# Attention feeding an FFN on one core: value loads ahead of plain casts, paired scores in the second batch, and a new set of order biases

## The chip, the cores and the metric

The kernel runs on one core of a Trainium2 chip. Times are device microseconds of one execution, lower is better. Every number comes from one profiled execution of the kernel before, from its run times, or from answers of its trace.

## The reference

Eight batches of eight heads, 576 positions, head size 64. Heads 0 to 3 attend to a plain window of 32, heads 4 to 7 to a window of 32 with steps of 4 ("dilated"). The result, laid out as tokens by 512 columns, goes through a two-layer FFN with a gate.

```python
mask_plain = (rel >= 0) & (rel < window)                       # window = 32
mask_dil = (rel >= 0) & (rel < window * dilation) & (rel % dilation == 0)   # dilation = 4
scores = np.where(masks, q @ k.T / 8, -1e9)
attn = softmax(scores)
x = (attn @ v).transpose(0, 2, 1, 3).reshape(4608, 512)
h = x @ w_in                                                   # 512 -> 2048
out = (h / (1 + np.exp(-beta * h))) @ w_out                    # 2048 -> 512
```

## The kernel before

Everything is an entry of a list of operations (`plan.op`). Each has the engines that may run it with a cost in ns, what it depends on, a due time `vt`, and the PSUM banks it takes. When all are listed, `Plan.run` plays them through a model: at each step it takes, for each engine, the operation with the smallest `vt` among those that could start nearly first, and writes it into that engine's program. `NUDGE` adds a bias in ns, by the number of the operation in the list, to the start that this choice compares. So the order on every engine is fixed when the program is built, and each engine then works through its own list, strictly in order. Where the model sees PE (TensorE) idle in the first 80 us, it puts in a matmul on zeros (`filler`, L1040), which keeps PE active.

A tile of the FFN is 512 tokens, a batch of attention 576, so nine tiles follow eight batches. For tile t, `slot_h` makes 16 blocks of h (L892, four matmuls of 512 columns each), tanh on ACT (L901) and the gate on DVE (L906); `block` multiplies by `w_out` (L927) and stores. Attention of batch b = t + 1 is spread between the FFN work of tile t by its due times.

How q, k and v of a batch get in depends on b:

- b = 0, 1, 2 (`b < DIRECT`): POOL's queue loads q and k as bf16 into `st`, PE transposes them (L474, L484), and ACT or DVE copies them to kT, qT (plain heads) and dk, dq (dilated heads).
- b = 3 to 7: POOL's queue casts q and k into scratch in DRAM (`cast`, four DMAs: k and q dilated, k and q plain), and SP's queue brings each back with a transposing DMA (`crossbar`, L465). A tiny copy on POOL, `pace` (L1006), holds all of this back until xT of batch b - 2 has arrived.
- The values: `direct_vd` loads the dilated heads' values (into `vd16`, or into `st` from b = 3), which the copy `spread` (L248) moves to vd, and twice a tail into `vt_`; `direct_vp` loads the plain heads' values into vp, after which the copy `halo` (L248) fills 32 rows of it. Either copy may stand on DVE, POOL or, for `spread`, ACT.

Scores are half-height matmuls (L688 dilated, L752 and L716 plain), and "T" is the tail of the dilated heads (L657). ACT takes exp (L624). For b = 0 the mask was added before by PE (L678, L738, L741), for others a multiply on DVE or POOL applies it (L628). Then come the values (L793 dilated, L809 plain, L778 the tail "U") and the normalisation on DVE (L643, L644) into xdm, xsp and xdt. For b = 0 and 1 PE transposes the result into xT; from b = 2 (`BY_DMA`) SP stores it to DRAM rows (L511, L519, L524) and fetches it with a transposing DMA into xT, in two halves (L538).

From b = 2 (`PAIRED`) one score operation handles two heads or pairs of heads; from b = 3 (`AT_ONCE`) all plain scores are one.

In `loads`, for b >= 3, the due times put the four casts at b - 2 to b - 1.97 and the values at b - 1.98 and b - 1.97:

```python
for n, (z, h0) in enumerate(((0, 4), (1, 4), (0, 0), (1, 0))):
    c = cast(b, z, h0, [go], b - 2 + .01 * n)
...
ld[b]["vd"] = direct_vd(b, [go] + war(*key), b - 2 + .02, [go] + war(("vt", b % 2)))
ld[b]["vp"] = direct_vp(b, [go] + war(("vp", b % 2)), b - 2 + .03)
```

On POOL's queue a batch of this kind is: k dilated, q dilated, k plain, vd, two vt, q plain, vp.

Of the kernel before, what the change touches and what calls it, by code (L numbers as in the profile page):

```python
# [39 lines left out]
class Plan:  # L40
# [3 lines left out]

    CAPS = {"h": 3, "p": 4, "o": 2, "z": 4, "a": 8, "s": 5, "w": 6}
    SWITCH = 95
    NUDGE = {10: 900, 16: -150, 32: -150, 34: 400, 40: -900, 65: -150, 99: -150, 121: -900, 159: -400,
        165: -400, 190: -150, 215: 400, 222: -400, 362: 900, 382: -900, 422: -900, 426: -150,
        443: 900, 537: 400, 553: -400, 656: -150, 836: 400, 838: 400, 881: -150, 914: -60,
        1113: 400, 1133: -900, 1136: 400, 1158: -400}  # L50
    LAT = {"PE": 210, "ACT": 45, "DVE": 45, "POOL": 60, "SP": 0}
    NEAR = {"PE": 40, "ACT": 60, "DVE": 60, "POOL": 60, "SP": 0}

# [3 lines left out]
    def op(self, engs, fn, deps=(), vt=0.0, acquire=None, group=None, dma=0, lat=None, halves=False, sbuf=False):  # L57
        acquire = acquire if acquire is None or isinstance(acquire, list) else [acquire]
        o = Op(engs, fn, deps, vt, acquire, group or acquire, dma, lat, halves, sbuf)
        o.bias = self.NUDGE.get(len(self.ops), 0)  # L60
        self.ops.append(o)
# [128 lines left out]
def kernel(  # L190
# [12 lines left out]
    B, H, S, D = q.shape  # L203
# [20 lines left out]
    DV = 80  # L224
    DIRECT = 3
    ADDED = 1
    PAIRED = 2
    BY_DMA = 2
    APART = 4
    AT_ONCE = 3  # L230
# [12 lines left out]
    def bank(g, dt=FP32):  # L243
        b = BANKS[g.bank][:]
        return b if dt == FP32 else b.bitcast(BF16)
# [50 lines left out]
    vd = [const([P, 4, C, DV], BF16, f"vd{i}") for i in range(2)]  # L296
    vt_ = [const([2 * KTL, 2, 4, DV], BF16, f"vt{i}") for i in range(2)]
# [38 lines left out]
    fill3 = plan.op([("DVE", 500)], t_fill3, vt=-7.8)  # L336
# [61 lines left out]
    def dma(queue, out, in_):  # L398
        {"POOL": nc.gpsimd, "SP": nc.sync}[queue].dma_start(out=out, in_=in_)  # L399

    def load(queue, args, deps, vt, kb, rate=.4, issue=750, lat=1100):
        return plan.op(
            [(queue, issue)],
            lambda e: dma(queue, *args), deps, vt, dma=kb * 1024 / rate / 1000, lat=lat)

    def direct_qk(b, z, h0, deps, vt):
        rows, n, dst = ((2 * GD, RD, std) if h0 else (P, RP, stp))
        src = bass.AP(tensor=(k, q)[z].tensor, offset=(k, q)[z][b, h0].offset,
                      ap=[[n * D, rows], [2 * S * D, 2], [1, n * D]])
        return load("POOL", (dst[z], src), deps, vt, 576, .41 if b else .33, lat=1100 if b else 1000)  # L410

    def first_keys():

        stage = g_t[1][0:2 * GD, 0:6, :].rearrange("p f n -> p (f n)").bitcast(FP32).rearrange("p (x e) -> p x e", x=2)
        src = bass.AP(tensor=k.tensor, offset=k[0, 4].offset,
                      ap=[[RD * D, 2 * GD], [2 * S * D, 2], [1, RD * D]])
        o = load("SP", (stage, src), [], -9.1, 576, .41, 400, 1200)
        return [plan.op([("ACT", 175 + .834 * RD * D), ("DVE", 160 + 1.042 * RD * D)],
                        lambda e, x=x: copy(e, std[0][:, x], stage[:, x]), [o], -9.1, sbuf=True) for x in range(2)]

    def direct_vp(b, deps, vt):

        out = []
        rows = vp[b % 2][:].rearrange("p (h i) d -> p h i d", h=4)
        for hs in ((slice(0, 4),) if b else (slice(0, 2), slice(2, 4))):
            n = hs.stop - hs.start
            src = bass.AP(tensor=v.tensor, offset=v[b, hs.start].offset, ap=[[D, QT], [QT * D, n * NI], [1, D]])
            o = load("POOL", (vp[b % 2][WIN:P, hs.start * NI:hs.stop * NI, 0:D], src), deps, vt, n * 144, .27,
                     1150 if b else 750, 1100 if b < DIRECT else 5500)

            def halo(e, hs=hs):
                copy(e, rows[0:WIN, hs, 1:NI, 0:D], rows[QT:P, hs, 0:NI - 1, 0:D])
            out.append(plan.op([("DVE", 160 + .27 * n * 320), ("POOL", 170 + 1.04 * n * 320)], halo, [o],
                               b - 1 if b else -2.5, sbuf=True))
        return out

    def direct_vd(b, deps, vt, tdeps=()):
        src = v[b, 4:8].rearrange("h (t T) d -> t h (T d)", T=C)[0:P]
        out = [load("POOL", (vd16_of[b].rearrange("p h T d -> p h (T d)"), src), deps, vt, 512, .35, lat=1100 if b < DIRECT else 4000)]
        for c in range(2):  # L440
            src = bass.AP(tensor=v.tensor, offset=v[b, 4].offset + ((P - WIN) * C + c) * D,
                          ap=[[2 * D, 2 * KTL], [S * D, 4], [1, D]])
            out.append(load("POOL", (vt_[b % 2][:, c, :, 0:D], src), list(tdeps), vt + (1.255 if b == 0 else .02 if b < DIRECT else 0) + .001 + .001 * c, 96, .2, lat=1100 if b < DIRECT else 4000))
        return out

    scratch = {}
# [1 line left out]
    def cast(b, z, h0, deps, vt):  # L448

        dst = scratch[b, z, h0] = dram_pool.tile([S * 4 * D], BF16, name=f"s{b}_{z}_{h0}")  # L450
        src = (k, q)[z][b, h0:h0 + 4]
        if h0:
            args = [x.rearrange("(a c e) -> c a e", c=16, e=1024) for x in (dst[:], src.rearrange("h s d -> (h s d)"))]
        else:
            args = (dst[:].rearrange("(s h d) -> s h d", h=4, d=D), src.rearrange("h s d -> s h d"))
        return load("POOL", args, deps, vt, 576, .38 if h0 else .2, 500 if h0 else 1700)
# [37 lines left out]
    def war(*keys):  # L494
        return [o for key in keys for o in last.get(key, ())]
# [4 lines left out]
    def wrote(*keys):  # L500
        for key in keys:
            last[key] = []
# [39 lines left out]
    def attention(b, ld, names, vts):  # L542
# [106 lines left out]
        for name in [n for n in names if n[0] in "ST"]:  # L649
# [19 lines left out]
            x = int(name[1])  # L669
            if b >= PAIRED and x % 2:  # L670
                continue
            xs = (x, x + 1) if b >= PAIRED else (x,)
            gs = [Group("s") for _ in range(2 * len(xs))]
# [279 lines left out]
    ld = {b: {} for b in range(B)}  # L953
    for n, (z, h0) in enumerate(((0, 4), (1, 4), (0, 0), (1, 0))):
        ld[0]["qk", z, h0] = first_keys() if n == 0 else direct_qk(0, z, h0, [], -9 + .01 * n)
    ld[0]["vd"] = direct_vd(0, [], -8.5, [fill3])
    ld[0]["vp"] = direct_vp(0, [fill3], -8.4)
    for n, (c0, c1) in enumerate(((0, 512), (512, 1024), (1024, 2048))):
        o = load("POOL", (w_in_bf[:, :, c0:c1], moe_w_in[:, c0:c1].rearrange("(c p) d -> p c d", p=P)),
# [11 lines left out]
    def t_identf(e):  # L971
# [6 lines left out]
        out=beta_half[:], in_=bank(gb)[:, 0:NFB], scalar=0.5, op=ALU.mult), [bt], -1.4, group=gb)  # L978
# [8 lines left out]
    def xready(lo, hi, kts=range(NKT)):  # L987
        return [o for ks, a, b, o in xcopy if a < hi and b > lo and set(kts) & set(ks)]

    def loads(b):  # L990
        if b < DIRECT:
            base = -7.25 if b == 1 else .2
            for n, (z, h0) in enumerate(((0, 4), (1, 4), (0, 0), (1, 0))):
                ld[b]["qk", z, h0] = direct_qk(b, z, h0, war(("st", z)), base + .01 * n)
            wrote(("st", 0), ("st", 1))
            ld[b]["vd"] = direct_vd(b, war("vd16"), base + .05, war(("vt", b % 2)) + [fill4])
            wrote("vd16", ("vt", b % 2))
            ld[b]["vp"] = direct_vp(b, war(("vp", b % 2)) + [fill4], base + .06)
            wrote(("vp", b % 2))
        else:  # L1000
            behind = [ld[b - 1]["x", z, h0] for z in range(2) for h0 in (0, 4)] if b > DIRECT else []

            mid = (b - 2) * S + S // 2

            def t_pace(e, b=b, mid=mid):
                nc.gpsimd.tensor_copy(out=pace[:], in_=(  # L1006
                    xT[0:1, 0, mid - 1:mid + 1] if b - 2 >= BY_DMA else g_t[b % 2][0:1, 0, 0:2]))
            go = plan.op([("POOL", 150)], t_pace, behind + (
                xready(mid - 1, mid + 1) if b - 2 >= BY_DMA else gop[b - 2, 0]), b - 2.4)
            for n, (z, h0) in enumerate(((0, 4), (1, 4), (0, 0), (1, 0))):  # L1010
                c = cast(b, z, h0, [go], b - 2 + .01 * n)
                key = [(((("dk", "dq") if h0 else ("kT", "qT"))[z]), b % 2, i) for i in range(2)]
                ld[b]["x", z, h0] = crossbar(b, z, h0, [c] + war(*key), b - 2 + .01 * n)
                wrote(*key)
            key = [("st", z) for z in range(2)] if b < DIRECT + 2 else [("st", b % 2)]
            ld[b]["vd"] = direct_vd(b, [go] + war(*key), b - 2 + .02, [go] + war(("vt", b % 2)))
            wrote(("st", b % 2), ("vt", b % 2))
            ld[b]["vp"] = direct_vp(b, [go] + war(("vp", b % 2)), b - 2 + .03)
            wrote(("vp", b % 2))

    steady = LATER.split()
    for t in range(NTT):
# [4 lines left out]
        b = t + 1  # L1027
# [46 lines left out]
```

## Time and profile before

| | us |
|---|---|
| median of three runs | 302.39 |
| the three runs | 512.2, 301.24, 302.39 |
| the profiled execution, its own time | 302.39 |
| its span, first to last instruction | 300.7 |
| PE busy | 294.7 |
| fillers on PE (L1040, 65 matmuls) | 11.0 |
| DVE busy, ACT busy, POOL busy | 183.2, 171.3, 90.5 |

The span is what the trace covers; the execution's own time holds some start and end besides. A row of the trace gives start, duration, engine, line, operation and tiles, and in brackets how long the engine stood idle before it and what ended that.

### The profile page before, as it was taken

To read this page: it belongs to the slowest core of one execution; us is meant where nothing else is said; L and a number is where in the kernel's file an instruction comes from. 1 tells how busy PE (TensorE), PEld (TensorE's weight loads), DVE (VectorE), ACT (ScalarE), POOL (GpSimd) and SP (SyncE) were. 2 spreads that over 40 slices of the span, in tenths; PEclk is the share of its full clock that TensorE was granted. 3 is DMA by queue.
4 is the path that set the end of the run, shared out by engine and by line. 5 is a ranking of instruction groups with operands and counts; after the bars stand their busy time and mean duration, and the time that the engine had idled before them with its cause. 6 is when DMAs were issued, how large, how long until landed. Compare 5 with 4: busy or idle time off the path is not lost.

```text
span 300.7 us, 6078 instructions
## 1 busy us (share of the span) xinstructions
PE 294.7 (98%) x2342; PEld 150.2 (50%) x2342; DVE 183.2 (61%) x415; ACT 171.3 (57%) x311; POOL 90.5 (30%) x130
## 2 busy tenths in 40 slices
PE   8999999999999989999999999999999999999995
PEld 5765556445554435544444544455444444444454
DVE  4769778787858716886477746685781543343300
ACT  3868864857457643865585546754852554555311
POOL 8997363852127204600733074110000000000000
PEclk9999999999999999999999999999999999999999
DMA  8999999799979998999899989996024000100122
GB/s 168 184 211 201 207 190 207 114 143 171 201 201 149 161 161 207 180 148 230 148 191 147 211 164 161 163 183 170 0 74 116 36 36 35 37 35 35 57 85 70
DMA packets 111248, 41.98 MB, mean 140 GB/s; under 512 B 87620, under 2 KB 104596, under 8 KB 111220
## 3 DMA queue, kind: packets, MB, share of 16 engines
q0 software_dynamic: 60336, 18.58, 60.1%
q1 hardware_dynamic: 50740, 22.95, 37.9%
q8 instruction: 18, 0.29, 0.4%
q10 hardware_dynamic: 144, 0.07, 0.1%
q14 instruction: 10, 0.08, 0.1%
HBM read 37.76 MB, written 18.87 MB: 188 GB/s over the span
## 4 chain that ended last, share of the span: by engine, by line
PE 83%; DMA 9%; POOL 2%; SPq 2%; issue 1%; DVE 1%; ACT 0%; POOLq 0%
PE bank L892 36%; PE bank L927 35%; DMA vp<-in_v_dram 6%; PE bank L1040 2%; DMA xT<-x 2%; PE bank L809 1%; PE bank L793 1%; PE bank L688 1%; SPq L465 1%; DMA x<-xsp 1%; PE bank L716 1%; PE bank L484 1%; PE bank L474 1%; PE bank L752 1%; POOL s L399 1%
## 5 line engine op out<-in xcount | busy, mean ns | idle before, releaser
L927 PE MATMUL bank<-w_out_bf,g 128*128 128x512 bf16 (+2 forms) x608 | 140.2, 368 | 0.0
L901 ACT ACTIVATE tnh<-bank,beta_half 128x512 bf16<-128x512 f32 x144 | 98.1, 689 | 71.2 <-PE bank L892 67.6
L906 DVE SCALAR_TENSOR_TENSOR g<-tnh,bank 128x512 bf16<-128x512 bf16 x144 | 97.2, 685 | 66.6 <-ACT tnh L901 66.0
L892 PE MATMUL bank<-xT,w_in_bf 128*128 128x512 bf16 (+1 forms) x584 | 137.6, 376 | 0.0
L892 PEld LDWEIGHTS <-w_in_bf 128*128 128x128 bf16 x584 | 55.4, 98 | 61.5
L927 PEld LDWEIGHTS <-g 128*128 128x128 bf16 x608 | 55.0, 98 | 56.2
L942 ACT ACTIVATE osb<-bank 128x512 f32<-128x512 f32 (+1 forms) x34 | 20.0, 589 | 32.8 <-PE bank L927 32.0
L624 ACT ACTIVATE pt<-bank 128x384 bf16<-128x384 f32 (+1 forms) x54 | 20.4, 465 | 5.3 <-PE bank L716 3.2
L624 ACT ACTIVATE ptd<-bank 128x512 bf16<-128x512 f32 x32 | 16.8, 604 | 4.8 <-PE bank L688 4.7
L644 DVE TENSOR_TENSOR xsp<-bank,rcp 96x384 bf16<-96x384 f32 x32 | 17.7, 554 | 1.1
L628 DVE TENSOR_TENSOR pt<-pt,mask_n 128x384 bf16<-128x384 bf16 (+1 forms) x39 | 13.0, 349 | 7.0 <-ACT pt L624 6.5
L643 DVE RECIPROCAL rcp<-bank 96x6 f32<-96x6 f32 (+2 forms) x72 | 12.9, 179 | 6.8 <-PE bank L809 3.4
L399 POOL DMA_DIRECT2D vp<-in_v_dram x9 | 15.2, 1695 | 1.3 <-DMA vp<-in_v_dram 1.3
L1006 POOL COPY pace<-xT 1x2 bf16<-1x2 bf16 x4 | 0.7, 176 | 47.7 <-DMA xT<-x 47.7
L628 DVE TENSOR_TENSOR ptd<-ptd,mask_d 128x512 bf16<-128x512 bf16 x27 | 11.0, 423 | 5.8 <-ACT ptd L624 5.0
L644 DVE TENSOR_TENSOR xdm<-bank,rcp 128x256 bf16<-128x256 f32 x32 | 13.6, 424 | 1.1
L399 POOL DMA_DIRECT2D s<-in_q_dram x10 | 13.6, 1358 | 0.0
L399 POOL DMA_DIRECT2D vt<-in_v_dram x16 | 13.3, 1000 | 0.0
L1040 PE MATMUL bank<-zero 128*128 128x256 bf16 x65 | 11.0, 314 | 1.1 <-DVE warm L307 1.1
L399 POOL DMA_DIRECT2D s<-in_k_dram x10 | 11.1, 1106 | 1.5 <-issue 1.1
L809 PEld LDWEIGHTS <-pt 128*128 128x128 bf16 x192 | 8.9, 97 | 4.9 <-DVE pt L628 0.2
L944 DVE TENSOR_SCALAR osb<-bank 128x512 f32<-128x512 f32 (+2 forms) x4 | 2.1, 525 | 14.5 <-PE bank L927 14.5
(111 smaller groups left out, 182.7 us busy)
## 6 DMA issues: line engine op xcount, KB each, us to landing
out_dram<-osb SPq DMA_DIRECT2D x35, 256.0 KB, 2.5
s<-in_k_dram POOLq DMA_DIRECT2D x10, 288.0 KB, 6.7
s<-in_q_dram POOLq DMA_DIRECT2D x10, 288.0 KB, 10.0
w_out_bf<-in_moe_w_out_dram POOLq DMA_DIRECT2D x2, 1024.0 KB, 16.2
vp<-in_v_dram POOLq DMA_DIRECT2D x7, 288.0 KB, 17.1
st<-in_q_dram POOLq DMA_DIRECT2D x6, 288.0 KB, 12.9
x<-xsp SPq DMA_DIRECT2D x12, 144.0 KB
st<-in_k_dram POOLq DMA_DIRECT2D x5, 288.0 KB, 14.2
```

The source lines that it names most:

```text
L399: {"POOL": nc.gpsimd, "SP": nc.sync}[queue].dma_start(out=out, in_=in_)
L624: nc.scalar.activation(out=w(), in_=sc(), func=ACT.Exp, scale=SCALE)
L628: E[e].tensor_tensor(out=w(), in0=w(), in1=m(), op=ALU.mult)
L643: nc.vector.reciprocal(out=r, in_=p[..., D])
L644: nc.vector.tensor_tensor(out=dst, in0=p[..., 0:D], in1=r.unsqueeze(len(p.shape) - 1).to_broadcast(list(p.shape[:-1]) + [D]), op=ALU.mult)
L809: nc.tensor.matmul(pv[:, a, h2, :], lhsT=lhs, rhs=vp[kv][:, (2 * x + h2) * NI + 3 * j + a, 0:D + 1], start=True, stop=True)
L892: nc.tensor.matmul(bank(g)[:, a:z], lhsT=w_in_bf[:, kt, fb * P:(fb + 1) * P], rhs=xT[:, kt, xo + a:xo + z], start=(i == 0 and kt == kts[0] ...
L901: nc.scalar.activation(out=th[:, 0:n], in_=bank(g)[:, 0:n], func=ACT.Tanh, scale=beta_half[:, fb:fb + 1])
L906: nc.vector.scalar_tensor_tensor(out=g_t[t % 2][:, fb, c0:c0 + n], in0=th[:, 0:n], scalar=1.0, in1=bank(g)[:, 0:n], op0=ALU.add, op1=ALU.mult)
L927: nc.tensor.matmul(bank(g)[:, lo:hi], lhsT=g_t[t % 2][:, fb, tb * P:(tb + 1) * P], rhs=w_out_bf[:, fb, lo:hi], start=(fb == 0), stop=(fb = ...
L942: nc.scalar.mul(out=ob[:, lo:hi], in_=bank(g)[:, lo:hi], mul=0.5)
L1040: nc.tensor.matmul(BANKS[b][:, 0:256], lhsT=zero[:, 0:P], rhs=zero[:], start=True, stop=True)
```

## The change

Four edits:

1. `NUDGE` is replaced: 30 biases of up to 900 ns become 110 of up to 2500 ns.
2. `PAIRED` goes from 2 to 1, so that the scores of b = 1 are made in pairs too. This also renumbers the operations that come after.
3. In `loads`, for b >= 3, the due times of the two plain casts grow by .03, to b - 1.95 and b - 1.94, past the values at b - 1.98 and b - 1.97.
4. In batch 0 the vd load's due time goes from -8.5 to -8.985, and the constant for the tails grows by .485, so that their own due time stays.

```diff
-    NUDGE = {10: 900, 16: -150, 32: -150, 34: 400, 40: -900, 65: -150, 99: -150, 121: -900, 159: -400,
...
+    NUDGE = {7: -900, 16: -2500, 17: -150, 19: -2500, 32: -400, 36: 900, 55: 900, 57: 900, 58: -2500,
+        70: 400, 71: 900, 81: -150, 85: -2500, 89: -2500, 94: -150, 113: -150, 114: -150,
...
-    PAIRED = 2
+    PAIRED = 1
...
-... vt + (1.255 if b == 0 else .02 if b < DIRECT else 0) + .001 + .001 * c, 96, .2, ...
+... vt + (1.7399999999999993 if b == 0 else .02 if b < DIRECT else 0) + .001 + .001 * c, 96, .2, ...
...
-    ld[0]["vd"] = direct_vd(0, [], -8.5, [fill3])
+    ld[0]["vd"] = direct_vd(0, [], -8.985, [fill3])
...
-                c = cast(b, z, h0, [go], b - 2 + .01 * n)
+                c = cast(b, z, h0, [go], b - 2 + .01 * n + (0 if h0 else .03))
```

What comes out on POOL's queue in the changed program, by batch (line numbers of the changed kernel are ten higher from the planner on):

| b | order of the loads after pace |
|---|---|
| 3 | q dilated, k dilated, vd, vt, vt, vp, k plain, q plain |
| 4 | k dilated, q dilated, vt, vt, vp, k plain, q plain, vd |
| 5 | q dilated, k dilated, vd, vt, vp, k plain, q plain, vt |
| 6 | k dilated, q dilated, vd, vt, vt, vp, k plain, q plain |
| 7 | k dilated, q dilated, vd, vt, vp, k plain, q plain, vt |

The copies move as well: in b = 4 the halo copy of vp goes from DVE to POOL and the spread copy of vd from POOL to DVE, where it stands ahead of the masks of that batch. On SP, qT's transpose of b = 3 now comes ahead of both stores of xsp of b = 2 instead of between other stores. In the opening POOL builds add_d and issues the vd load of b = 0 ahead of ident_b.

## The prediction

> **What bounds the kernel now.** I read the page's parts 1 and 2 first, then the waits of PE (TensorE), the chain of waits around the one PE wait that is not in the opening, DVE's timeline there, and last the DMA share of that stretch.
>
> ```profile
> span 300.7 us, 6078 instructions
> PE 294.7 (98%) x2342; PEld 150.2 (50%) x2342; DVE 183.2 (61%) x415; ACT 171.3 (57%) x311; POOL 90.5 (30%) x130
> ...
> PEclk9999999999999999999999999999999999999999
> DMA  8999999799979998999899989996024000100122
> ...
> PE bank L793 <- DVE ptd L628: 1.3, 1, 1.3
> PE bank L1040 <- DVE warm L307: 1.1, 1, 1.1
> PE bank L678 <- POOL add_d L350: 0.3, 1, 0.3
> ```
>
> PE is the bound, at full clock. Because the ends of matmuls are modelled, 98% alone proves little, so I laid PE's own instruction order end to end: columns / 2.4 ns plus 2.5 for a wide matmul (four of 512 columns take 0.86 us in the chain of waits), the spacing of starts in the timeline for the narrow ones, and 95 ns wherever half-height scores meet full-height work (0.97 instead of 0.86 us after each score). The sum puts the last matmul at 294.4 us; the trace has it at 297.4. The 3.0 us of difference arise in two places: 2.0 in the first 17 us, and 1.4 at 111 to 113 us. Elsewhere PE never waits. Besides, 65 matmuls on zeros (L1040, 11.0 us busy) fill gaps that the planner expected. That is all there is to win.
>
> The second place, by the chain of waits and then the timelines of DVE and PE:
>
> ```profile
> 87.80 0.18 POOL pace L1006
> ...
> 93.65 18.19 DMA vp<-in_v_dram
> ...
> 111.86 0.48 DVE vp L248
> 112.34 0.03 issue
> 112.38 0.44 DVE ptd L628
> ...
> 109.09 0.43 DVE L628 TENSOR_TENSOR ptd<-ptd,mask_d 128x512 bf16<-128x512 bf16 x1 [2.98 <-ACT ptd L624]
> 111.86 0.48 DVE L248 COPY vp<-vp 32x1280 bf16<-32x1280 bf16 x1 [2.35 <-DMA vp<-in_v_dram]
> 112.38 1.10 DVE L628 TENSOR_TENSOR ptd<-ptd,mask_d 128x512 bf16<-128x512 bf16 x3
> 112.86 0.30 PE L793 MATMUL bank<-vd,ptd 128*128 128x65 bf16 x4 [1.28 <-DVE ptd L628]
> ```
>
> The reader is to see a queue effect. PE waits for a mask, the mask for nothing but DVE, and DVE stands 2.35 us in the halo copy of vp, whose DMA is the last of its batch on POOL's queue and lands 18.19 us after its issue. Three masks wait behind it. The batch is b = 4.
>
> ```profile
> q0 software_dynamic: 8608, 1.84, 86.5%
> q1 hardware_dynamic: 6746, 2.20, 56.6%
> ```
>
> These are the DMA queues between 88 and 113 us: POOL's queue (q0) and SP's (q1) together fill the engines (packets overlap, so the shares add to over 100%). Moving a transfer ahead makes another late.
>
> **What the Trainium skill says.** Perfetto Trace Analysis, section Tensor Engine Instruction: ACT, DVE and GpSimd queues are strict FIFO. The rows above agree: three masks start at 112.38, after the copy. DMA: Bandwidth & Descriptors, Issuing engines are not separate DMA queues: transfers of SP and POOL share 16 engines and interleave. The two shares above agree. The same page, Queues, rings and completion order: on one engine, one ring's descriptors are consumed in order. The issue-to-landing times of b = 4 agree: k plain 89.36 + 8.9 = 98.3, vd 90.46 + 9.6 = 100.1, q plain 92.55 + 13.4 = 106.0, vp 93.65 + 18.2 = 111.8. TensorE: Matmul & The Clock Gate, Back-to-back issue gap, gives 131 ns for 512 columns sustained; here 216 is measured, and I use that.
>
> **The change, part by part.** I compared the two instruction orders engine by engine.
>
> *PE.* The same matmuls but for the fillers: 65 become 61. The half-height blocks are 26 in both orders, so 52 edges of 95 ns stay, although the scores of b = 1 are now paired: pairing merges blocks, the new order splits others. PE: -4 x 0.107 = -0.43 us.
>
> *The wait at 111 us.* In b = 4 the vp load goes from last to fourth on POOL's queue (behind two dilated casts and two vt), and its halo copy from DVE to POOL. By the table above it takes about k plain's place, landing near 99 to 101, ten us before need. The wait goes: 0.86 us after 110.56 PE would have gone on at 111.42, and it went on at 112.86, so -1.4 us.
>
> *What is late next.* In b = 4 the biases put the vd load (256 KB into st) last, behind both plain casts, and the spread copy of vd now stands on DVE ahead of the T mask and all four ptd masks. It is the same trap with another load. POOL's queue carries the same packets, so its end is at 111.8 less two things: the batch starts about 0.7 us earlier (qT of b = 3 no longer stands between the xsp stores, so I put pace at 87.1 instead of 87.8), and kT's transpose now waits for a later cast, so q0 runs longer without a rival, worth 1.5 to 3 us. So vd lands at 108 to 110.5. The matmuls of U (L778), now first, stand at 107.1 in the laid order, plus the 2.25 us by which PE trails it there: 109.4. They need the landing, 0.42 (spread), 0.28 (mask) and some 0.05: U could start at 108.8 to 111.2. Bounds 0 to 2.0 us; I take 0.6, nearer the early end because kT is out of the way.
>
> *Plain casts last (b = 3 to 7).* q plain lands later, up to vp's old place: 111.8 - 106.0 = 5.8 us later. Behind it on SP: qT's transpose (3.5 us of queue), the stores of x, xT of the batch before; xT releases POOL's pace of the next batch and the matmuls of the next FFN tile. In b = 4 qT was issued at 107.78 and landed 5.9 later, 113.7; its scores began at 117.0, so 3.3 us of cover, less the 1.7 that PE is ahead if no wait comes. With q0 quicker as above q plain is late by 1 to 2 us, not 5.8. xT's cover is thinner: in before the second xT of b = 3 releases pace at 116.38 and tile 3 begins at 118.7. Bounds 0 to 2.5 us over the four turns; I take 0.2.
>
> *Opening.* POOL now makes add_d and issues a vd load (1.00 us) before ident_b: 1.36 + 0.79 + 1.00 + 0.95 (add_d) + 0.35 (ident_f) + 0.73 (k load) + 0.55 gives 5.7, where L678 started at 5.42: +0.3. k and q plain of b = 0 land about 1.2 us later behind vd, which nine fillers ahead of the first scores hide; if they don't, the first scores of b = 0 (L752) wait for the qT copies, up to +1.0. The other end is -0.3, since values of b = 0 come earlier. I take +0.3.
>
> *Rest.* b = 1 in pairs: the same eight exps and masks, at nothing, hidden by ACT and DVE at 5 to 8 tenths. Masks of b = 2 on POOL, six of 0.72 us instead of one, end about 1 us before the T copy of b = 3 is due; without that cover 0.5 us. pace of b = 3 about 2 us earlier (its gate is, by PE's order): no gain by itself.
>
> **Sum:** -0.43 - 1.4 + 0.6 + 0.2 + 0.3 = -0.7 us. The profiled execution took 302.39 us with a span of 300.7, so 1.7 lies around it; it is also the median run. Span 300.0, time 301.7 us.
>
> **Rivals.**
> - *Clean:* vd lands by 108.6 and every xT keeps its cover. For it: q0 without a rival is quick; k plain and vp have the same 2304 rows, and k plain took 2.2 us (q dilated lands at 88.62 + 7.5 = 96.1, k plain at 98.3), vp 5.8 beside the transposes. Against it: the 86.5% share. -0.43 - 1.4 - 0.3 to +0.3: 300.3 to 300.9 us.
> - *The wait is only exchanged:* vd lands at 110.5 to 111.5 and one or two xT come 1 to 2 us late. For it: same queue, same last place, same DVE trap. 302.5 to 306 us.
> - *The loop turns slow (the other side):* q plain takes vp's old place in full. Its price is 5.8 - 3.3 = 2.5 us at the first batch, and because qT, xT and pace follow one another on SP it is paid again in b = 5, 6 and 7: +10, about 311 us. It decides from the point where q plain is late by more than the 3.3 us of cover. Against it: after 200 us the DMA row falls to 0, so the loop has room at its end, and in b = 5 qT was issued at 133.78, so some 15 us before its scores were due by PE's order (155.5).
> - *Faster by over 2%* would need 6 us; the order holds 1.8 us of gain plus 2 of opening. Only an odd measurement gives it.
>
> **How the numbers follow.** Forecast (301 to 302.5) 0.46, clean 0.20, exchanged 0.20, loop 0.12, faster 0.02. About 2% is what a measurement of this kernel can tell from no change. So faster 0.02, same 0.86, slower 0.12. Lower end: clean, 300.3, less 0.6 for the scatter (half the distance of the two lower runs, 301.24 and 302.39): 299.7. Upper end: all bounds at their worst, -0.4 - 1.4 + 1.0 + 2.0 + 2.5 = +3.7: 306.1. The loop's 0.12 and small tails stay out.
>
> **What would show it.** Right: no DVE wait for vp near 111; if PE waits in b = 4, DVE's idle time names the st load and a vd copy; last matmul of the laid order about 2 to 3 us late. Wrong: PE rows waiting for xT or for kT and qT in several batches (loop), PE idle for over 1 us ahead of L752 in the first 15 us (opening), or a vp wait that is still there (the change does not do what it says).

## The result, and the profile after

The changed kernel takes 303.44 us in the median, the kernel before 302.32: a ratio of 1.0051 (95% interval 1.0034 to 1.0068). It is slower, by 1.0 to 2.1 us, where 0.7 us faster was forecast; the range of 299.7 to 306.1 holds it. The profiled execution took 302.73 us with a span of 300.9. Executions more than 1.5% above the fastest of their kernel are in no ratio: 512.2 us of before, 343.35 and 438.66 of after, and below 306.6 of open_of_before, 306.12 and 306.52 of first82_before, 308.09 of first82_after and 307.79 of after_unpaired.

The page of after, in the lines that answer to those of before, and its list of PE's waits (line numbers are ten higher):

```profile
span 300.9 us, 6004 instructions
PE 292.0 (97%) x2299; PEld 150.3 (50%) x2338; DVE 184.9 (61%) x413; ACT 170.5 (57%) x310; POOL 93.7 (31%) x133
...
PEclk9999999999999999999999999999999999999999
DMA  8999999799899997999999989985240000100122
```
```profile
PE bank L937 <- issue: 1.3, 8, 0.2
PE bank L1050 <- DVE warm L317: 1.1, 1, 1.1
PE bank L688 <- POOL ident_b masks.py:199: 0.4, 1, 0.4
PE bank L762 <- ACT qT L258: 0.3, 1, 0.3
PE bank L871 <- DVE xsp L654: 0.2, 1, 0.2
PE bank L803 <- DVE xdm L654: 0.2, 1, 0.2
PE bank L667 <- DVE dkt L258: 0.2, 1, 0.2
PE bank L484 <- DMA st<-in_q_dram: 0.2, 1, 0.2
```

The wait of 1.3 us for ptd is gone. There are now six waits of 0.2 to 0.4 us with a releaser, all of them in the first 18 us; the one for ident_b stands where before had 0.3 us for add_d. (2338 weight loads but 2299 matmuls: 39 matmul records are missing, so PE's busy time is not compared; times below are starts. The first line, eight gaps of 0.16 us for which the trace shows no releaser, is not read as a wait either.)

DVE's timeline of after around the old wait:

```profile
108.53 0.18 DVE L258 COPY qt<-dq 64x128 bf16<-64x128 bf16 x1
108.63 0.41 DVE L258 COPY vd<-st 128x1024 bf16<-128x1024 bf16 x1
110.26 0.29 DVE L638 TENSOR_TENSOR ptt<-ptt,mask_t 96x256 bf16<-96x256 bf16 x1 [1.22 <-ACT ptt L634]
110.81 0.42 DVE L638 TENSOR_TENSOR ptd<-ptd,mask_d 128x512 bf16<-128x512 bf16 x1 [0.27 <-ACT ptd L634]
```

The copy of vd stands ahead of the masks as foreseen, but it starts at once, since vd landed at 107.8 (landings here are those of a transfer's last packet, unless the release is named; the chain of waits counts 0.3 to 1.3 us more, up to the release), and the T mask then waits for ACT's exp, not for the copy. The queues between 88 and 113 us carry nearly what they carried before:

```profile
q0 software_dynamic: 8608, 1.84, 84.0%
q1 hardware_dynamic: 7220, 2.61, 63.8%
```

So where did the time go? PE's timeline of the opening, a few rows of before and then of after:

```profile
8.63 0.48 PE L484 MATMUL bank<-ident_b,st 64*64 64x64 bf16 x36
10.41 0.48 PE L484 MATMUL bank<-ident_b,st 64*64 64x64 bf16 x36
12.02 0.30 PE L752 MATMUL bank<-qT,kT 64*128 64x96 bf16 x6
17.71 0.59 PE L892 MATMUL bank<-xT,w_in_bf 128*128 128x512 bf16 x2
```
```profile
10.79 0.48 PE L494 MATMUL bank<-ident_b,st 64*64 64x64 bf16 x36
12.96 0.48 PE L494 MATMUL bank<-ident_b,st 64*64 64x64 bf16 x36
14.18 0.54 PE L762 MATMUL bank<-qT,kT 64*128 64x96 bf16 x12 [0.25 <-ACT qT L258]
18.86 0.38 PE L902 MATMUL bank<-xT,w_in_bf 128*128 128x512 bf16 x1
```

The plain k and q come later because POOL issues their loads later: vd and add_d now stand ahead of them. POOL's rows of before and then of after:

```profile
2.97 0.74 POOL L399 DMA_DIRECT2D st<-in_k_dram  x1
3.70 0.73 POOL L399 DMA_DIRECT2D st<-in_q_dram  x1
```
```profile
2.18 0.77 POOL L409 DMA_DIRECT2D vd<-in_v_dram  x1
4.17 0.73 POOL L409 DMA_DIRECT2D st<-in_k_dram  x1
5.44 0.84 POOL L409 DMA_DIRECT2D st<-in_q_dram  x1
```

The plain k (the load into st from in_k) is issued 1.2 us later and the plain q 1.7. On PE the transposes of the plain k and q (two groups of 36) start 2.2 and 2.6 us later, the first plain scores 2.2 us later, and the first h, with which the FFN begins, 1.15 us later. Nothing after it gives that back, except that the wait at 111 us is gone. In both orders 48 fillers stand ahead of the first h, so none of this is a difference in fillers.

Worked out from the starts as in the prediction, as the distance of PE from its own order laid end to end, after trails by 3.2 us at the first h, by 4.0 at 45 us and by 3.6 at the end; before by 1.9, 2.0 and, after the wait at 111 us, 3.0. With after's order 0.43 us shorter that is the 0.2 us between the two spans. The medians differ by 1.1 us, so one profile of each was not the whole story.

### The profile page after: what moved, and what is told of

Its sections match the earlier page's. It is cut to its first block, busy times and chain, and to the rows that moved or that the text cites. A ratio compares the mean times of both kernels' runs of the same rounds, so it can differ in the third digit from the quotient of the medians.

```text
span 300.9 us, 6004 instructions
## 1 busy us (share of the span) xinstructions
PE 292.0 (97%) x2299; PEld 150.3 (50%) x2338; DVE 184.9 (61%) x413; ACT 170.5 (57%) x310; POOL 93.7 (31%) x133
## 4 chain that ended last, share of the span: by engine, by line
PE 92%; DVE 2%; DMA 2%; issue 1%; ACT 1%; DVEq 0%; POOLq 0%
PE bank L902 41%; PE bank L937 40%; PE bank L819 2%; DMA st<-in_q_dram 2%; PE bank L698 1%; PE bank L803 1%; PE bank L726 1%; PE bank L484 1%; PE bank L1050 1%; PE bank L494 1%; PE bank L788 1%; PE bank L762 1%; DVE pt L638 1%; PE bank L871 0%; PE bank L667 0%
## 5 line engine op out<-in xcount | busy, mean ns | idle before, releaser
L937 PE MATMUL bank<-w_out_bf,g 128*128 128x512 bf16 (+2 forms) x586 | 138.2, 367 | 2.1 <-issue 1.3
L902 PE MATMUL bank<-xT,w_in_bf 128*128 128x512 bf16 x567 | 137.7, 376 | 0.8
L952 ACT ACTIVATE osb<-bank 128x512 f32<-128x512 f32 (+1 forms) x32 | 18.8, 587 | 36.9 <-PE bank L937 36.8
L654 DVE TENSOR_TENSOR xsp<-bank,rcp 96x384 bf16<-96x384 f32 x32 | 17.7, 554 | 1.1
L638 DVE TENSOR_TENSOR pt<-pt,mask_n 128x384 bf16<-128x384 bf16 (+1 forms) x38 | 14.0, 396 | 7.0 <-ACT pt L634 6.6
L653 DVE RECIPROCAL rcp<-bank 128x4 f32<-128x4 f32 (+2 forms) x72 | 12.9, 179 | 6.7 <-PE bank L819 3.6
L638 DVE TENSOR_TENSOR ptd<-ptd,mask_d 128x512 bf16<-128x512 bf16 x26 | 11.2, 445 | 3.7 <-ACT ptd L634 3.2
L954 DVE TENSOR_SCALAR osb<-bank 128x512 f32<-128x512 f32 (+2 forms) x6 | 3.5, 577 | 13.5 <-PE bank L937 13.5
L409 POOL DMA_DIRECT2D s<-in_k_dram x10 | 11.2, 1122 | 0.6 <-issue 0.6
L409 POOL DMA_DIRECT2D vp<-in_v_dram x9 | 10.2, 1130 | 1.4 <-DMA vp<-in_v_dram 1.4
## 6 DMA issues: line engine op xcount, KB each, us to landing
vp<-in_v_dram POOLq DMA_DIRECT2D x7, 288.0 KB, 10.5
```

Source lines behind the costliest of these rows:

```text
L638: E[e].tensor_tensor(out=w(), in0=w(), in1=m(), op=ALU.mult)
L653: nc.vector.reciprocal(out=r, in_=p[..., D])
L654: nc.vector.tensor_tensor(out=dst, in0=p[..., 0:D], in1=r.unsqueeze(len(p.shape) - 1).to_broadcast(list(p.shape[:-1]) + [D]), op=ALU.mult)
L902: nc.tensor.matmul(bank(g)[:, a:z], lhsT=w_in_bf[:, kt, fb * P:(fb + 1) * P], rhs=xT[:, kt, xo + a:xo + z], start=(i == 0 and kt == kts[0] ...
L937: nc.tensor.matmul(bank(g)[:, lo:hi], lhsT=g_t[t % 2][:, fb, tb * P:(tb + 1) * P], rhs=w_out_bf[:, fb, lo:hi], start=(fb == 0), stop=(fb = ...
L952: nc.scalar.mul(out=ob[:, lo:hi], in_=bank(g)[:, lo:hi], mul=0.5)
```

## The experiments

In all but two of them the choice of the planner is replaced by written-out lists, one per engine, of the numbers of the operations (-1 is a filler). With the lists of before or after this gives that kernel's order on every engine, and a change of a list moves just that in the order. One thing can move besides: the PSUM bank (where a matmul puts its result) is still chosen by the planner's model. Some spliced kernels have a wait of PE that can only be one for a bank, because the matmul reads nothing of what it waits for, and none of these stands in the four profiles of the two kernels themselves: for `DVE g` 0.4 us in open_of_before (at 29 us), 0.5 and 0.7 in open_before_vd_early (at 41 and 137) and 0.2 in after_open_but_pool (at 41), for `ACT osb` 0.7 in before_casts_last (at 147). Differences of this size in these kernels are not the order's alone.

```diff
-                first = min(s + o.bias for s, o, _ in c)
-                s, o, d = min((x for x in c if x[0] + x[1].bias <= first + self.NEAR[e]), key=lambda x: (x[1].vt, x[0]))
+        queues = {e: list(q) for e, q in FORCED.items()}
...
+                o = self.ops[q[0]]
```

Ratios are to the kernel before, measured beside each; "first h" is the start of PE's first h in the profiled execution.

| kernel | median us | ratio, 95% interval | first h |
|---|---|---|---|
| after_again | 303.62 | 1.004, 1.002 to 1.006 | 19.6 |
| open_of_before | 302.32 | 1.0007, 0.9989 to 1.0026 | 18.2 |
| first82_before | 302.95 | 1.003, 1.0005 to 1.0056 | 18.4 |
| first82_after | 303.16 | 1.0033, 1.0017 to 1.0049 | 18.5 |
| before_again | 302.29 | 1.0002, 0.9978 to 1.0025 | 18.2 |
| before_vp_early | 301.52 | 0.9976, 0.9958 to 0.9994 | 18.1 |
| after_vd_early | 303.38 | 1.0045, 1.0028 to 1.0063 | 19.2 |
| open_before_vd_early | 302.1 | 1.0004, 0.9981 to 1.0028 | 18.4 |
| after_pool_before | 305.53 | 1.0097, 1.0072 to 1.0122 | 22.3 |
| after_open_but_pool | 303.35 | 1.0052, 1.0033 to 1.007 | 19.0 |
| before_paired | 302.47 | 1.001, 0.9994 to 1.0027 | 18.2 |
| first82_vd_early | 302.7 | 1.0007, 0.9988 to 1.0027 | 17.8 |
| before_open_after | 303.67 | 1.0059, 1.0036 to 1.0081 | 19.8 |
| before_casts_last | 302.94 | 1.0038, 1.0025 to 1.0052 | 18.3 |
| first82_vd_early_2 | 301.98 | 1.0002, 0.9987 to 1.0017 | 18.6 |
| after_unpaired | 303.6 | 1.0052, 1.0035 to 1.0069 | 20.0 |
| after_ident_first | 303.23 | 1.0045, 1.0023 to 1.0068 | 19.1 |
| before_vd_second | 302.75 | 1.0046, 1.0025 to 1.0066 | 19.0 |

### Opening or late part: splices in time

The changed kernel once more, and three splices. Theory A is that the time is lost in the opening and in batch 1, theory B that it is lost in the late loop. On POOL the heads of the lists differ so (16 and 18 are the dilated and plain q, 17 the plain k, 19 vd, 7 add_d, 32 and 2 the two identities, 22 vp); the other engines' lists are cut at the same time:

```diff
     "POOL": [
-        16, 19, 7, 32, 17, 2, 18, 22,
+        16, 32, 2, 17, 18, 7, 19, 22,
```

after_again:

> The changed kernel once more, as the base of the comparison and for a second profile. Theory A (opening and batch 1): about 1.0 us slower than before, and the second profile shows PE trailing its own order by about 3.2 us at 17 us and by about 4.2 at 46 us, then no more loss; no wait at 111 us. Theory B (late loop): the same time, but this profile shows PE waits after 85 us (for the vd copy or for xT) that the first profile happened not to have, 1 us or more in all.

open_of_before:

> The changed kernel, but everything that starts before the first h of tile 0 (about 18 us) is in the order of the kernel before, on all five engines; the rest keeps the order of after. Theory A: the opening's 1.2 us come back, 1.2 us faster than after, 302.2 (about level with before). Theory B: the opening is hidden later anyway, no change against after (303.4).

first82_before (before's lists up to 82 us, after's from there):

> Before's order on every engine up to 82 us, after's order from there (casts last, vp's copy on POOL, vd's copy on DVE). Theory A: all of the gain and none of the loss: 302.3 - 1.4 = 300.9. Theory B: all of the loss: 303.4 or more.

first82_after:

> The converse: after's order up to 82 us (with its opening and its paired scores of batch 1), before's from there, with its vp copy on DVE. Theory A: all of the loss and none of the gain: 302.3 + 1.2 + 0.8 - 0.4 (fewer fillers) = 303.9, and the wait at 111 us is back. Theory B: level with before or a little faster, 301.9 to 302.3.

The second profile of after trails by 3.9 us at the first h and by 4.6 at 45 us, and loses nothing later, as theory A said. Before's opening alone makes after 1.0 to 1.3 us faster (1.0007 against 1.004 in the same comparison and 1.0051 in the first): the opening is shown, and before_open_after below shows it from the other side. But the splices at 82 us fit neither theory: before's first part with after's late part should have gained 1.4 us and is 0.9 slower, and the converse lost 1.0 instead of 1.6. The late part's gain, which one profile had shown as 1.4 us, is not there in the medians.

The profile of first82_after shows why one profile misled. Its chain of waits, and its windows for PE (length, PE busy, granted clock, DMA share, GB/s):

```profile
92.72 21.29 DMA vp<-in_v_dram
114.01 0.02 issue
114.03 0.48 DVE vp L328
```
```profile
111.00:113.00 2.00, 1.66 (x12) 1.00 1.54 63
113.00:114.00 1.00, 0.00 (x0) 1.00 0.83 176
114.00:115.00 1.00, 0.00 (x0) 0.90 1.29 298
115.00:116.00 1.00, 0.97 (x6) 0.50 0.68 255
116.00:117.00 1.00, 1.00 (x4) 0.50 1.05 239
117.00:118.00 1.00, 1.00 (x18) 0.50 0.99 314
118.00:119.00 1.00, 1.00 (x6) 0.90 0.38 143
```

Here the same load of vp is there at 114.0, not at 111.8. PE waits 2.4 us instead of 1.3. The granted clock falls to 0.50 within the wait (0.90 as the mean of 114 to 115 puts the fall at 114.8) and is back 3.4 us later, at 118.2, which costs another 1.6; PE trails by 7.3 us afterwards instead of 3.3. The same happens with the new order. open_of_before's profiled execution took 306.6 us; only the place of its wait is read from it, from the list of waits and the chain:

```profile
PE bank L858 <- DVE ptt L708: 2.6, 1, 2.6
```
```profile
95.39 17.27 DMA st<-in_v_dram
112.66 0.02 issue
112.68 0.43 DVE vd L328
```

vd is there at 112.7, and U (here L858) waits for its mask behind the copy of vd: the exchanged wait exists, it just does not come every time. The mean granted clock of these two profiles is 0.994, and first82_before has six executions of 305.6 to 306.5 us at that same mean clock, while the rest have a median of 302.15: there too, by this sign, a long wait comes whole or not at all; the waits of these six were not profiled. In the two kernels themselves the sign is rare: no execution of after has it among the 34 that took under 340 us, and one of before among those measured beside (305.47 us).

### How large is the wait of b = 4

Before's list for b = 4 reads pace, k and q dilated, k plain, vd, vt, vt, q plain, vp; after's reads, behind pace too, k and q dilated, vt, vt, vp, k and q plain, vd. Theory C is that the last load of this list lands at times that differ by some us, rival D that the wait is 1.4 us every time. The first change makes before_vp_early, the second after_vd_early:

```diff
     "POOL": [
-        658, 659, 661, 663, 667, 668, 669, 665, 670,
+        658, 659, 661, 670, 663, 667, 668, 669, 665,
...
-        656, 658, 665, 666, 667, 660, 662, 664,
+        656, 658, 664, 665, 666, 667, 660, 662,
```

before_again (the kernel itself):

> The kernel before once more, for a second profile. Theory C (the last load of b = 4 on POOL's queue lands at times that differ from execution to execution by some us, so the wait for it is anything from 0 to 4 us): this profile's wait for the vp copy near 111 us differs from the 1.4 us of the first, and the time moves by the same amount. Rival D (the wait is 1.4 us every time): 1.3 to 1.5 again.

before_vp_early:

> The kernel before with one thing changed: in b = 4 the vp load stands third on POOL's queue (behind the two dilated casts) instead of last. All else, with the halo copy on DVE, is in before's order. Rival D: 1.4 us faster than before, 300.8. Theory C: faster by the mean of a wait that is often small, 0.5 to 1.0 us, 301.2 to 301.7, and the scatter upwards shrinks. If a later slack takes the wait up: 302.2.

after_vd_early:

> The changed kernel with one thing changed: in b = 4 the vd load stands third on POOL's queue instead of last (as the change has it in b = 3 and 6). Theory C (the new last load, vd, makes PE wait in some executions, as in the 4 us wait of the profile with the old opening): 0.3 to 0.7 us faster than after, 302.8 to 303.2, none above 304.5. Rival D (as in the two profiles of after, vd is never late): no change, 303.5.

open_before_vd_early (the second change on top of open_of_before):

> Both at once: the changed kernel with before's opening (up to 18 us) and with the vd load of b = 4 third on POOL's queue. Theories A and C: 1.2 us for the opening and 0.3 to 0.7 for vd, 301.6 to 302.0, a little faster than both kernels. Rival D: as with the opening alone, 302.3.

before_again, DVE around its vp copy:

```profile
109.76 0.43 DVE L628 TENSOR_TENSOR ptd<-ptd,mask_d 128x512 bf16<-128x512 bf16 x1 [3.77 <-ACT ptd L624]
110.22 0.48 DVE L248 COPY vp<-vp 32x1280 bf16<-32x1280 bf16 x1
```

No idle time stands before the copy: vp had landed at 107.8, and PE does not wait in b = 4. pace ran at 84.5 us here, at 87.8 in the first profile. So with before's late order the wait was 1.3 (first profile), 0 (before_again), 2.4 (first82_after), 1.3 (before_paired), 0 (before_open_after) and 0 us (before_vd_second). Theory C holds for the wait. Its other half does not: the profiled time moved by 0.17 us, from 302.39 to 302.22, and not by 1.3, because this execution came to the first h 0.5 us later and PE waited 0.4 us for another mask at 170 us. So the wait of one profile is not what the execution gains without it. Its mean is what before_vp_early removes: 0.24%, 0.7 us (0.2 to 1.3), with no execution above 302.44. It is the only kernel here that is faster than before by more than its interval.

The vd wait of after is rarer still: after_vd_early changes nothing that can be told apart (1.0045 against 1.004 and 1.0051), nor does vd early on top of before's opening (1.0004 against 1.0007; the profile of 303.24 us has 1.1 us of the waits for a bank). The 0.3 to 0.7 us expected for it was too much.

### Which part of the opening

Theory P is that POOL's order is what costs in the opening, theory E that the order on the other engines is.

after_pool_before (after's lists with POOL's opening of before) and its complement after_open_but_pool (PE, ACT, DVE and SP of before up to 18 us, POOL's opening of after); the POOL heads are those shown above:

> The changed kernel with POOL's opening alone in before's order (ident_f and ident_b first, the vd load of b = 0 behind k, q plain and add_d); PE, ACT and DVE keep after's order. Theory P (POOL's order is what costs the 1.2 us of the opening: ident_b, the dilated q and the plain loads come late): level with the kernel that has all of before's opening, 302.3. Theory E (the order on PE, ACT and DVE is what costs): 303.5 as after, or slower, since after's PE order asks for the values early.

> The complement: the changed kernel with before's order on PE, ACT, DVE and SP up to 18 us, but POOL's opening as in after. Theory P: 303.3 or more, nothing is won. Theory E: 302.3, as with all of before's opening.

The complement speaks for theory P: with POOL's new opening, before's order elsewhere wins nothing. The first kernel does not speak for E, because it made a new trap. Its DVE timeline:

```profile
11.99 0.57 DVE L328 COPY vd<-vd 128x1024 bf16<-128x1024 bf16 x1 [2.65 <-DMA vd<-in_v_dram]
12.49 0.34 DVE L328 COPY dkt<-dk 128x384 bf16<-128x384 bf16 x1
```

After's DVE order asks for vd early. With vd late again, dkt stands behind that copy, PE waits 2.1 us for dkt, and the granted clock is 0.79, 0.50 and 0.86 in the windows from 12 to 18 us. POOL's queue and the other engines' orders belong together, so a part of one put into the other is not a clean test.

Then the whole opening of after put into before (before_open_after, the reverse of the splice shown above), and two small moves inside POOL's list, the first in before (before_vd_second), the second in after (after_ident_first):

```diff
     "POOL": [
-        16, 32, 2, 17, 18, 7, 19, 22,
+        16, 19, 32, 2, 17, 18, 7, 22,
...
-        16, 19, 7, 32, 17, 2, 18, 22,
+        16, 32, 2, 19, 7, 17, 18, 22,
```

before_open_after:

> The kernel before with after's opening on all five engines up to 18 us, before's order from there. Theory A (opening costs about 1 us by itself): 303.0 to 303.3. If the opening costs only together with after's order of batch 1: 302.2. Overlap: with PE 1 us later the wait for vp in b = 4 gets shorter by as much, so 302.5.

before_vd_second:

> The kernel before with the vd load of b = 0 second on POOL's queue (behind the dilated q, ahead of the two identities and of k and q plain); all else as before. If issuing and carrying vd that early is what the opening loses: 0.5 to 1.2 us slower, 302.5 to 303.4, and the first h at 18.6 to 19.3 us instead of 17.6 to 18.5. If it is the other moves of the opening: 302.2.

after_ident_first:

> The changed kernel with ident_f and ident_b made ahead of the vd load and of add_d on POOL; the rest of POOL's queue and all other engines as in after. If PE's first wait (for ident_b, until 5.5 us) is what the opening loses: 0.5 to 0.7 us faster, 302.9, with the first h as much earlier. If what follows is bound by the dilated q, which lands 0.6 us later than in before because the vd load runs beside it: no change, 303.5.

One load moved ahead by five places gives before the loss of after: ratio 1.0046, first h at 19.0. Rows of its PE timeline:

```profile
6.56 1.02 PE L748 MATMUL bank<-add_d,ident_b 128*128 128x512 bf16 x4 [1.40 <-POOL add_d L420]
10.32 0.48 PE L554 MATMUL bank<-ident_b,st 64*64 64x64 bf16 x36 [0.57 <-DMA st<-in_k_dram]
```

The vd issue keeps POOL from making add_d, and the plain k lands at 10.0 us, against 7.5 and 8.4 in the two profiles of before and 9.8 and 10.3 in those of after. About half of this is the issue of vd on POOL: k is issued at 3.76 us instead of 2.97 and 2.98. The rest lies behind the issue: from there to the release k takes 6.5 us instead of 4.9 and 5.8. In after_ident_first ident_b is early and PE's first wait is gone, yet the time is that of after; but POOL now issues k later still (4.67 instead of 4.17), and the plain k and q land at 10.5 and 11.9, against 10.0 and 11.0 in the mean of after's two. So an early ident_b wins nothing while k and q come no earlier, and the two kernels together point to these loads; a kernel that changes ident_b alone was not run. The share of add_d in before_vd_second wasn't measured by itself either.

before_open_after loses 0.59% (1.1 to 2.4 us), more than expected, and the 302.5 us of an overlap with the wait for vp did not come. So with the opening of after, everything else that the change does to the order is worth no more than the difference between 1.0059 and 1.004 or 1.0051, which the intervals don't tell from nothing. PE does not wait for vp in its profile, but this doesn't show that a later PE hides the wait: vp landed at 109.4 here, and first82_after, with the same opening, waited 2.4 us.

### Pairing, and plain casts last

before_paired (pairs in before, `PAIRED` as in after) and after_unpaired (the reverse, shown; pairing shifts the numbers, and 223 in the paired list is the pair of 223 and 228, 232 is the old 233). Theory Q is that pairing makes the loss between 18 and 45 us.

```diff
-    PAIRED = 1
+    PAIRED = 2
...
     "PE": [
-        223, 232, 160,
+        223, 228, 233, 160,
```

> The kernel before with the scores of batch 1 in pairs as the one change (each pair at the place of its first half; everything else in before's order). The prediction put pairing at nothing: 302.2. Theory Q (pairs bring the exps and masks of batch 1 in lumps, and the values wait for masks; this is the 0.4 to 0.8 us that after loses from 18 to 45 us): 302.5 to 303.0. A gain by fewer edges between half-height and full-height work: 302.0.

> The changed kernel with the scores of batch 1 one by one again (both halves of a pair at the pair's place), all else in after's order. Theory Q (pairing makes the loss from 18 to 45 us): 0.3 to 0.8 us faster, 302.9. Pairing at nothing, as predicted: 303.5.

Neither differs from its base (1.001 with an interval across 1, and 1.0052 against 1.004 and 1.0051). Pairing costs and brings nothing here that can be told apart. What the profiles of after trail more between the first h and 45 us, 0.6 to 0.8 us against 0.1 to 0.3 in the profiles with before's order there, may in part be the four fillers that after has fewer in this stretch (0.43 us). No wait of over 0.15 us with a releaser stands there in either profile of after, and the rest isn't settled.

before_casts_last, in b = 3 to 7 alike (shown for b = 4):

```diff
     "POOL": [
-        658, 659, 661, 663, 667, 668, 669, 665, 670,
+        658, 659, 661, 667, 668, 669, 670, 663, 665,
```

> The kernel before with the one edit to the due times taken over on POOL's queue: in b = 3 to 7 the two plain casts go behind vd, vt and vp; every other queue is in before's order. If plain casts in last place cost nothing: 301.5, as with vp alone moved ahead in b = 4. Theory B (q plain and xT come late in b = 5 to 7 in a typical execution): 302.2 or more, with PE waits for qT, kT or xT in the profile.

It is 0.38% slower than before, although vp is no longer last in b = 4. PE's waits in its profile:

```profile
PE bank L758 <- DMA dq<-s: 1.0, 1, 1.0
...
PE bank L962 <- ACT osb L1012: 0.7, 1, 0.7
```

PE waits 1.0 us for the dilated q's transpose on SP in b = 4, which took 11.2 us from its issue here and 9.7 in the first profile of before, and not for qT, kT or xT of the later batches as theory B had it. The second wait is one for a bank and belongs to the splice. So the loss is measured, but its cause is shown for 1.0 us at most, in one profile (303.62 us, above its median). The edit to the due times is no gain alone.

### A version with both late traps removed

first82_vd_early and its second run (first82_before with vd third in b = 4, in before's numbers):

```diff
     "POOL": [
-        658, 659, 661, 668, 669, 670, 663, 665, 667,
+        658, 659, 661, 667, 668, 669, 670, 663, 665,
```

> Before's order up to 82 us, after's from there, with the vd load of b = 4 third on POOL's queue instead of last: the late part of the change without either trap. Theory C: the wait of b = 4 is gone, 301.5 as with only vp moved ahead in before, less 0.4 if fewer fillers count here; and no execution above 303.5, where the same kernel with vd last had six near 306. If plain casts behind the values cost anything in b = 5 to 7, more than 302.

> The kernel with before's first 82 us and vd early a second time, since its median (302.7) and its profiled execution (301.27, no wait after 82 us) differ by 1.4 us. If after's late part has a wait that comes in some executions: this profile shows it after 82 us. If the difference lies in the opening (loads that land at other times): PE's first h starts 0.5 to 1.4 us later than in the profile of 301.27, and nothing is lost after that.

Medians of 302.7 and 301.98, ratios of 1.0007 and 1.0002: level with before, and the 0.7 us of before_vp_early is not repeated. Both profiles (301.4 and 302.16 us; the 301.27 of the expectation is the lowest time, not the profiled one) show no wait after 82 us; they differ by 0.8 us in the first h (17.8 and 18.6), which is the second branch of what was expected. So the difference between these two executions is made in the first 18 us. The longest of its 28 executions took 304.2, where the same kernel with vd last has the six near 306: vd last in b = 4 is what makes those. What else in the late order takes the 0.7 us back stays open: PE waits for xT in two of the twelve profiles with it, 0.3 us in first82_before (at 145 us) and 0.2 in after_vd_early (at 146), and that is not enough.

## Why the prediction was wrong, by its own steps

Forecast were 0.7 us of gain, measured are 1.0 to 2.1 us of loss. Two steps make the difference, about equally: the opening, and the late part, which was to bring 1.0 us (-0.43 - 1.4 + 0.6 + 0.2) and with before's opening brings nothing (open_of_before, 0.3 us faster to 0.8 slower).

- **Opening, +0.3: the first step that failed.** The prediction saw vd ahead of k and q plain, put them 1.2 us late and let nine fillers ahead of the first scores (L752) hide it, with +1.0 if they didn't. The 1.2 us are the later issue of k alone; q is issued 1.7 us later, and both take longer behind vd. In the mean of the two profiles of each they landed 2.0 (k, 8.0 to 10.0) and 1.6 us (q, 9.4 to 11.0) later, up to the release 2.0 and 2.1, and the cover was none: the first scores moved by 2.2 us, and the first h by 1.15. The sign that the prediction named for this came, PE idle for 1.3 us ahead of the first plain scores, where before has 0.3, but in five pieces. Over all profiles the first h stands at 18.2 on average in the ten with before's opening (17.7 to 18.6) and at 19.3 in the six with after's (18.5 to 20.0). In time it is 1.0 to 1.3 us (open_of_before) or 1.1 to 2.4 (before_open_after), at or beyond the end of the bound. The fillers are no reserve when the chain that they bridge, from landing over transpose, copy and scores to the first h, is itself what is late.
- **The wait at 111 us, -1.4: right in place and mechanism, wrong in size.** The copy of vp on DVE blocked the masks, and moving vp removes it (before_vp_early). (vp goes to fifth place on POOL's queue, behind four loads, not to fourth.) But 1.4 was one execution's landing; over executions it is 0.7.
- **The sum of the late part.** Even these 0.7 us don't appear with the rest of the change around them: open_of_before stands at 1.0007, first82_before at 1.003, and with vd early as well open_before_vd_early at 1.0004 and first82_vd_early at 1.0007 and 1.0002. So it is not only the opening that eats the gain. What in the late order does is not shown.
- **vd late, +0.6.** The trap is real (2.6 us of wait in one execution), but after_vd_early shows nothing of it in the median. In after's two profiles vd was released at 108.1 and 111.2; the band given, in the same measure, was 108 to 110.5. The batch was not earlier by 0.7 us as assumed: pace ran at 87.5 and 90.0.
- **Plain casts last, +0.2.** Of the twelve profiles with after's late order none shows a wait for qT there and two show one for xT, of 0.3 and 0.2 us; the 2.5 us of the bound and the loop of the rivals did not come. In before's surroundings the same edit costs 0.38%, with a wait for the dilated q that no step named.
- **Fillers, -0.43, and pairing, 0.** Pairing holds. The four fillers lie between 18 and 45 us, where PE trails by about as much more. The blocks of half-height scores are 24 in the trace of before and 23 in those of after, not 26 in both; by the prediction's 95 ns an edge that is 0.2 us.
- **The starting sum.** The prediction's two places of loss in before, 2.0 and 1.4 us, add up to 3.4 and not to its 3.0. Elsewhere PE must come out ahead of the laid order by the rest, so that order is good to about half a us.

## What to carry to other kernels

A load moved ahead on a queue costs what stands behind it, and in an opening that is the chain that everything else starts from: price both its issue on the engine that issues the others too and its transfer (0.8 us, and 0.7 to 1.6 us, for the plain k in before_vd_second). A wait for a DMA at the end of a busy queue is a number with a spread; one profile gives one draw of it, so take a second profile before you put the whole wait into a sum. And a gain from a removed wait is a maximum, not a term: here 1.4 us in one profile were 0.7 with that load alone moved, and nothing that could be told apart with the rest of the new order around it.

## What the runs showed of the hardware

- The last load of b = 4 landed at 107.8, 108.7, 109.4, 111.5, 111.8 and 113.5 us in six executions with before's late order. Pace varied with it (84.5, 85.2, 86.7, 87.8, 86.2 and 86.9 us), but doesn't explain it: issued at 93.65 and 92.72, vp took 18.2 and 21.3 us up to the release. What makes the difference wasn't found.
- The price of a PE wait has a step. Idle for 1.3 us, PE went on at full clock (the first profile, before_paired). In three executions the clock fell to 0.50: in first82_after at 114.8 us, PE idle since 112.7; in open_of_before at 113.0, idle since 110.8; in after_pool_before at 13.15, where PE had been idle from 10.8 to 12.9. So 2.1 to 2.3 us of idle time were enough, and each time full clock came back 3.4 us after the fall. In first82_after the wait cost 4.0 us in all. The falls lie on a grid: by the clock records of the traces the stretch of full clock before them is 109.23 us in the first two and 6.83 in the third, 32 and 2 times 3.41 us. The Trainium skill, TensorE: Matmul & The Clock Gate, Part 1, has the two clocks, and the fall after an idle window of about 3.4 us that runs free of the program; the runs agree on the half clock, on the grid and on the time to recover, but PE need not be idle for a whole window: 2.1 us were enough. Between 1.3 and 2.1 us no run here shows which way it goes.
